# When the weights of the second half are loaded, and phi_q@KV in single tiles instead of pairs: a transformer block with kernel-feature attention

## The chip, the cores and the metric

The kernel runs on one core of a Trainium2 chip. A core has five engines that run side by side and meet through semaphores: TensorE (matmuls; in the profile PE, and PEld for its weight loads), VectorE (DVE), ScalarE (ACT), GpSimd (POOL) and SyncE (SP), which here issues nearly all DMA transfers. Matmuls write to PSUM, eight banks of 2 KB per partition; everything else lives in SBUF, 128 partitions wide. Sixteen DMA engines move the data between DRAM and SBUF, and also the engines' own instructions.

The metric is the device time of one execution in microseconds (us), the median over several executions. A change is called faster or slower against that median. TensorE's clock can be throttled; the profile gives the granted clock as a share of full speed.

## The reference

One sequence of 2048 rows, 640 wide; 32 heads of 20; FFN width 1536; bfloat16.

```python
qkv = layernorm(x) @ wqkv                     # -> q, k, v per head (32 heads of 20)
pq  = einsum("bhsd,hdf->bhsf", q, w_phi)      # the same for k -> pk
phi_q = concat([softmax(pq), softmax(-pq)])   # over f; the same for pk -> phi_k
kv  = einsum("bhsf,bhsd->bhfd", phi_k, v)     # sum over all 2048 rows
z   = einsum("bhsf->bhf", phi_k)
num = einsum("bhqf,bhfd->bhqd", phi_q, kv)
den = einsum("bhqf,bhf->bhq", phi_q, z) + 1e-6
h   = x + (num / den) @ wo
h2  = h + (gelu(layernorm(h) @ w_gate) * (layernorm(h) @ w_up)) @ w_down
```

The attention is linear: every row's phi_k and v are first summed into one small kv matrix per head, and only then can the first row's phi_q be multiplied with it.

## The kernel before, in words

The rows are cut into 16 tiles of 128, and four tiles make a block. The kernel has a first phase, which ends with the sum kv, and a second, which makes attention, W_o and the FFN.

**First phase.** w_phi is folded into the weights of k and q, so that pk and pq come from one matmul each (`fold`, tile names wa, Wk2, Wq2; the q weights come transposed from DRAM as WqT through `load_T`). A loop over the 16 tiles (`for t in range(NT)`) does in pass t: the matmuls pk of tile t and two exponentials on ACT (`k_tile`, E); the matmuls v of tile t+4 (`v_mm`, pv) and their copy out of PSUM on ACT (`v_ev`, vS); the layer norm of tile t+6 on ACT (`ln_ap`) and its transpose by a DMA that SP issues (LN1T); sums, reciprocals and products for phi_k on DVE and POOL (`k_norm`, vt). At passes 5, 9, 13 and 15 some tiles are added up in PSUM (`kv_tile`, kvp): 40 small matmuls of 32 columns each per tile. In pass 15 and behind it 6 tiles, 240 matmuls, stand in a row. Passes 7 to 10 also issue the five transposes of WqT, pass 9 three tiny DMAs (kmask), passes 10 to 14 the five folds for q. In pass 13 SP is given Wg, Wo and Wu, 1920, 800 and 1920 KB, each in one DMA. SP works its list in order: what waits there holds all that is behind it.

**Second phase.** `kv_mask` moves the sum from PSUM to SBUF (KV). Wd, 1920 KB, is issued by SP in two DMAs as soon as the memory of the first phase is free. Blocks of pq (`q_mm`) and their exponentials (`q_exp`, Eq) go on, woven by hand with the attention of tiles 0 and 1. The attention of a tile has stages: `attn_a_mm` (phi_q@KV, 40 matmuls of 32 rows, PSUM tile ab, and the copies to AB), `attn_b`, `attn_b2`, `attn_b3` (divide, on POOL and DVE: pr, den, rd, w, tt, o; then a DMA transpose oT), `attn_c` (po, times Wo), `attn_d` and `attn_d2` (the sum with x, statistics), `attn_e` (layer norm, DMA transpose LN2T).

`weave(units, stages)` sets the order: units are TensorE's long work, `gate_up` (10 matmuls gu, 2.2 us at 512 columns, gelu on ACT, product GT on DVE) and `down` (12 matmuls pd, the sum y on DVE, later a store). A stage with the number i is put ahead of unit i; what lies beyond the last unit goes to the next weave with the number reduced. The second weave has 16 units, the third 20.

From stage 12 of the second weave (`split`) on, the eight PSUM banks are given out one by one in a ring (`bank`): ab takes four, a gu two, a po two, a pd one. Tiles 8 to 15 go through `attn_pair`: ab of two tiles, eight banks, and then the copies of both, two on ACT and two on DVE for each tile. The AB buffers are four.

TensorE's and SP's instructions stay in the order in which they are written; so do those of the other engines (`manual_schedule`).

Of the kernel before, what the change touches and what calls it, by code (L numbers as in the profile page):

```python
# [17 lines left out]
def kernel(  # L18
# [12 lines left out]
    nc = tc.nc  # L31
# [8 lines left out]
    NC = D // P  # L40
    NF = FF // P
# [16 lines left out]
    KC = Dh + 2  # L58
# [3 lines left out]
    QH, QF = H // 4, D // 4  # L62
# [19 lines left out]
    Wo = const.tile([P, NC, D], BF16, name="Wo")  # L82
    Wg = const.tile([P, NC, FF], BF16, name="Wg")
    Wu = const.tile([P, NC, FF], BF16, name="Wu")
    KV = const.tile([P, 2, SL, KC], BF16, name="KV")

    Eq = [const.tile([P, len(g), 2, 512], BF16, name=f"Eq{j}") for j, g in enumerate(QG)]
# [109 lines left out]
    wo_v = A_wo.rearrange("(c p) n -> p c n", p=P)  # L197
    wg_v = B_w_gate.rearrange("(c p) n -> p c n", p=P)
    wu_v = B_w_up.rearrange("(c p) n -> p c n", p=P)
# [68 lines left out]
    def ln_ap(t, on_act=False, on_pe=False):  # L268
        ln = (ln_act if on_act else ln_dve)(p1, "1", *lnp[t])
        if on_pe:  # L270
            lnp[t] = ln
        else:
            transpose_to(LN1T[t // 4][:, :, t % 4 * P:(t % 4 + 1) * P], ln, False)
# [15 lines left out]
    def v_mm(t, us=(0, 1)):  # L289
        if 0 in us:  # L290
            pv[t] = gtile("pv")
        proj(pv[t], t, Wv, us)
# [19 lines left out]
    def k_tile(t):  # L312
        pk = gtile("pk")
        proj(pk, t, Wk2, rows=t == 0)
        Ek[t] = ev.tile([P, 2, D], BF16, name="E", bufs=8)
        for s in range(2):
            nc.scalar.activation(Ek[t][:, s, :].rearrange("p (u f) -> p u f", u=2), pk[:, :, 0:HD],  # L317
                                 ACTF.Exp, scale=((lnp[t][2], nrstd[t]) if t in CT else (1.0, -1.0))[s])
# [45 lines left out]
    def q_mm(j, part=(0, 1)):  # L364

        if 0 in part:
            pqs[j] = gtile("pq")
        for i, bc in enumerate(QG[j]):
            if i not in part:
                continue  # L370
            b, c = divmod(bc, NC)
            for kc in range(NC):
                nc.tensor.matmul(pqs[j][:, i, :], lhsT=Wq2[:, kc, c * P:(c + 1) * P], rhs=LN1T[b][:, kc, :],  # L373
                                 start=(kc == 0), stop=(kc == NC - 1))

    def q_exp(j, signs=(0, 1)):
        for s in signs:
            nc.scalar.activation(Eq[j][:, :, s, :], pqs[j][:, 0:len(QG[j])], ACTF.Exp, scale=(1.0, -1.0)[s])  # L378
# [80 lines left out]
    ev_cm = tc.tile_pool(name="ev", bufs=1, side="right", reuse_waits="tile")  # L459
    ev = ev_cm.__enter__()  # L460

    for t in range(NT):
        if t == T3:
            ps_cm.close()
            psG = ps_cm.enter_context(tc.tile_pool(name="psG", bufs=3, space=PSUM, reuse_waits="tile"))
            psK = ps_cm.enter_context(tc.tile_pool(name="psK", bufs=1, space=PSUM, reuse_waits="tile"))
            kvp = psK.tile([P, 2 * SL, VC], F32, name="kvp")
        k_tile(t)
        if t == 0:
            ln_ap(6)  # L470
        if t in FQ:
            fold(WqT, Wq2, True, [i for i, f in enumerate(FQ) if f == t])
        for j in range(len(QT)):
            if t == QT[j]:
                q_mm(j)
                q_exp(j)
        for i in KVG.get(t, ()):
            kv_tile(i)
        if 0 < t < NT - 4:
            v_mm(t + 4)  # L480
        if t > 0 and t + 6 < NT:
            ln_ap(t + 6, on_act=True)
        if 0 < t < NT - 4:
            v_ev(t + 4)
        if t % 2 == 0 and t + 8 < NT:
            ln_st(t + 8, t + 9)
        k_norm(t)
        load_T(WqT, 0, *[i for i, f in enumerate(LQ) if f == t])
        if t == 10:
            transpose_to(LN1T[0][:, :, P:2 * P], ln_a(1), False)  # L490
        if t == 12:
            ln_ap(0, on_act=True)
        if t == 7:
            nc.gpsimd.memset(kmask[QUAD[0]], 1.0)
            for k, lo, n, base in ((3, 0, 2, 0), (2, 6, 3, 12)):
                m = kmask[QUAD[0], lo:lo + 6].rearrange("p (k n) -> p k n", k=k)
                nc.gpsimd.affine_select(out=m, in_=m, pattern=[[4, k], [-Dh, n]],
                                        compare_op=ALU.is_ge, fill=0.0, base=base, channel_multiplier=1)
                nc.gpsimd.affine_select(out=m, in_=m, pattern=[[-4, k], [Dh, n]],
                                        compare_op=ALU.is_ge, fill=0.0, base=Dh - 1 - base, channel_multiplier=-1)  # L500
        if t == 8:
            nc.gpsimd.memset(KV, 0.0)
        if t == 9:
            for r in (1, 2, 3):
                nc.sync.dma_start(kmask[QUAD[r]], kmask[QUAD[0]])
        if t == 11:
            nc.gpsimd.tensor_copy(KV[:, 0, :, KC - 1], kmask)
            nc.gpsimd.tensor_copy(KV[:, 1, :, 0], kmask)
        if t == 13:
            nc.sync.dma_start(Wg, wg_v)  # L510
            nc.sync.dma_start(Wo, wo_v)
            nc.sync.dma_start(Wu, wu_v)
    q = len(QT)
    for t in range(12, NT):
        kv_tile(t)
# [9 lines left out]
    p2r = ctx.enter_context(tc.tile_pool(name="p2r", bufs=1, side="right", reuse_waits="tile"))  # L525
    Wd = p2r.tile([P, NF, D], BF16, name="Wd")
    wd_v = B_w_down.rearrange("(c p) n -> p c n", p=P)
    for f in (0, NF // 2):
        nc.sync.dma_start(Wd[:, f:f + NF // 2], wd_v[:, f:f + NF // 2])

    ABs = [p2r.tile([P, 2, H, KC], F32, name=f"AB{i}") for i in range(2)]
    ABs += [LN1F[:, i * 2 * H * KC:(i + 1) * 2 * H * KC].rearrange("p (s h f) -> p s h f", s=2, h=H) for i in range(2)]
    LN2T, st = {}, {}
# [9 lines left out]
    def attn_a_mm(t):  # L543

        b = t // 4
        if b not in LN2T:
            LN2T[b] = p2.tile([P, NC, 512], BF16, name="LN2T", bufs=2)
        if psB:
            ab = [bank("ab") for r in range(4)]
        else:  # L550
            st[t, "ab"] = gtile("ab"), gtile("ab")
            ab = [x[:, i] for x in st[t, "ab"] for i in range(2)]
        for s in range(2):
            for c in range(NC):
                i, h, n = SLOT[c]
                h += s * QH
                for r, q in enumerate(QUAD):
                    nc.tensor.matmul(ab[r][:, h * KC:(h + n) * KC], lhsT=eq(t, c, s)[q],  # L558
                                     rhs=KV[q, s, i:i + n].rearrange("p h f -> p (h f)"),
                                     start=(s == c == 0), stop=(s == 1 and c == NC - 1), skip_group_check=True)  # L560
        st[t] = ab

    def attn_pair(t):

        for i in (t, t + 1):
            attn_a_mm(i)
        for i in (t, t + 1):
            AB = ABs[i % len(ABs)]
            for r in range(4):
                (nc.scalar.copy, nc.vector.tensor_copy)[r % 2](  # L570
                    AB[:, :, r * QH:(r + 1) * QH].rearrange("p s h f -> p s (h f)"),
                    st[i][r][:, 0:2 * QH * KC].rearrange("p (s x) -> p s x", s=2))
            st[i] = AB

    def attn_a(t, dve=0):
        attn_a_mm(t)
        AB, ab = ABs[t % 2], st[t, "ab"]
        for u in ((1, 0) if t in (4,) else (0, 1)):
            (nc.vector.tensor_copy if u >= 2 - dve else nc.scalar.copy)(
                AB[:, :, u * UH:(u + 1) * UH].rearrange("p s (r h) f -> p r s (h f)", r=2),  # L580
                ab[u][:, :, 0:2 * QH * KC].rearrange("p r (s x) -> p r s x", s=2))
        st[t] = AB

# [178 lines left out]
    q_mm(q + 2)  # L762
    attn_t(0)
    q_exp(q + 1, (1,))
    q_exp(q + 2, (0,))
    q_mm(q + 3, (0,))
    attn_b(1, True)
# [30 lines left out]
    def attn_at(t, i, offs):  # L798

        fns = (attn_a, attn_b, attn_b2, attn_b3, attn_c, attn_d, attn_d2, attn_e)  # L800
        return [(i + o, fn, t) for fn, o in zip(fns, offs) if o >= 0]

    SHORT = (0, 2, 3, 4, 9, 9, 10, 12)
# [3 lines left out]
    def attn_rest(t, i):  # L807
        return [(i + o, fn, t) for fn, o in zip((attn_b, attn_b2, attn_b3, attn_c, attn_d, attn_d2, attn_e), LONG)]
# [4 lines left out]
          attn_at(2, 0, (-1, 0, 1, 2, 7, 7, 8, 10)) + attn_at(3, 1, (2, 3, 4, 5, 9, 9, 10, 12)) + attn_at(4, 6, SHORT2) + attn_at(5, 9, SHORT2) +  # L813
          attn_at(6, 13, SHORT2))
    weave(gus(0, 256, 512) + downs(0, (2, 3)),
          attn_at(7, 0, SHORT) + [(12, split), (14, attn_pair, 8), (16, attn_pair, 10)] + attn_rest(8, 15) +
          attn_rest(9, 17) + attn_rest(10, 19) + attn_rest(11, 21))
    weave(gus(1, 0, 512) + downs(1, range(4)),
          [(18, attn_pair, 12), (20, attn_pair, 14)] + attn_rest(12, 19) + attn_rest(13, 21) + attn_rest(14, 23) +
          attn_rest(15, 25))  # L820
    for b in (2, 3):
        weave(gus(b, 0, 512) + downs(b, range(4)), [])
# [31 lines left out]
```

## Time and profile before

| | |
|---|---|
| median of 3 runs | 282.93 us (282.88 to 282.96) |
| the profiled execution | 283.22 us, of which the span from first to last instruction is 281.2 us |
| TensorE busy | 270.1 us (96%), mean granted clock 0.987 |
| DVE, ACT, POOL busy | 173.7, 140.4, 96.4 us (62%, 50%, 34%) |
| DMA | 21.46 MB, mean 76 GB/s |
| Wg, Wo, Wu from issue to landing | 9.3, 10.5, 14.8 us |
| Wd, each of two | 7.9 us |
| LN1T, oT, LN2T, each | 2.6 us |

How to read it: the profile names each instruction by engine, line and operation, with output tile <- inputs. "Idle before" is the engine's idle time ahead of an instruction, and after "<-" stands what ended it; "issue" means that nothing the profile shows was being waited for. The slices cut the span in 40 equal parts with the busy share in tenths. The chain of waits goes back from the last instruction to what released it. Matmuls are pipelined and their recorded lengths overlap, so the starts are the better measure. SPq is the time in which SP issued; the transfer follows it.

### The profile page before, as it was taken

The page shows a single profiled execution, that of the slowest core. Times are in us where ns is not written, and L with a number is a line of the kernel's source. Part 1 is how long each engine was busy: PE and PEld are TensorE (multiplying, and loading weights), DVE is VectorE, ACT ScalarE, POOL GpSimd, SP SyncE. Part 2 cuts the span into 40 slices and gives each one's busy share as a digit, 9 for nine tenths or more (in the row PEclk, how much of TensorE's full clock was granted, in tenths as well). Part 3 has the DMA queues.
Part 4 walks back from the last instruction along what each step waited for, and adds up shares of the span by engine and source line. Part 5 has one row for each costly group of instructions (what it writes and reads, how often), then busy time and mean ns, then how long its engine had stood idle before and what let it go on. Part 6 is the DMA issues. An engine that isn't in the chain of part 4 may idle for free.

```text
span 281.2 us, 7231 instructions
## 1 busy us (share of the span) xinstructions
PE 270.1 (96%) x2981; PEld 172.7 (61%) x2995; DVE 173.7 (62%) x332; ACT 140.4 (50%) x241; POOL 96.4 (34%) x218
## 2 busy tenths in 40 slices
PE   7999999998499999999999999999999999999996
PEld 3777777765145688778864555576455567444574
DVE  5899999995068586666558785327776432233232
ACT  5789897887069975545534245404234520222200
POOL 4248898764001123736411383201255210000000
PEclk9999999999689999999999999999999999999999
DMA  7972627699900011324220322210113411000011
GB/s 200 193 244 47 73 57 112 72 233 392 357 7 2 2 24 26 72 50 94 43 55 2 70 48 47 49 48 28 47 23 72 48 47 49 23 0 0 2 47 47
DMA packets 42401, 21.46 MB, mean 76 GB/s; under 512 B 35201, under 2 KB 40577, under 8 KB 42369
## 3 DMA queue, kind: packets, MB, share of 16 engines
q1 hardware_dynamic: 41712, 20.98, 30.9%
q8 instruction: 23, 0.38, 0.6%
q10 hardware_dynamic: 656, 0.03, 0.2%
q14 instruction: 10, 0.07, 0.1%
HBM read 10.18 MB, written 2.62 MB: 46 GB/s over the span
## 4 chain that ended last, share of the span: by engine, by line
PE 87%; DVE 4%; DMA 3%; issue 3%; ACT 2%; SPq 0%; POOL 0%; POOLq 0%
PE gu L692 37%; PE pd L711 19%; PE pq L373 8%; PE po L632 8%; PE pk L284 5%; PE pv L284 4%; PE kvp L351 2%; PE ab L558 2%; DMA Wv<-in_A_wqkv_dram 2%; DMA LN1T<-ln 1%; DVE stats L113 1%; PE wa L237 1%; DVE y L714 1%; ACT vS L304 1%; ACT E L317 1%
## 5 line engine op out<-in xcount | busy, mean ns | idle before, releaser
L695 ACT ACTIVATE g<-gu 128x512 bf16<-128x512 f32 (+1 forms) x60 | 30.7, 512 | 67.7 <-PE gu L692 66.9
L698 DVE TENSOR_TENSOR GT<-gu,g 128x512 bf16<-128x512 f32 (+1 forms) x60 | 34.4, 580 | 48.2 <-PE gu L692 39.3
L692 PE MATMUL gu<-LN2T,Wg 128*128 128x512 bf16 (+1 forms) x291 | 61.3, 335 | 0.5
L692 PE MATMUL gu<-LN2T,Wu 128*128 128x512 bf16 (+1 forms) x300 | 61.8, 336 | 0.0
L711 PE MATMUL pd<-Wd,GT 128*128 128x320 bf16 (+2 forms) x396 | 53.5, 295 | 0.0
L711 PEld LDWEIGHTS <-GT 128*128 128x128 bf16 x396 | 37.9, 98 | 14.6 <-DVE GT L698 0.2
L692 PEld LDWEIGHTS <-Wu 128*128 128x128 bf16 x300 | 29.3, 98 | 22.6
L692 PEld LDWEIGHTS <-Wg 128*128 128x128 bf16 x300 | 28.8, 98 | 21.2
L284 PEld LDWEIGHTS <-LN1T 128*128 128x128 bf16 x290 | 27.8, 98 | 10.7 <-DMA LN1T<-ln 0.2
L714 DVE TENSOR_TENSOR y<-pd,x_sb 128x320 bf16<-128x320 f32 (+2 forms) x29 | 13.9, 480 | 29.0 <-PE pd L711 29.0
L332 POOL TENSOR_TENSOR vt<-vS,rs 128x672 bf16<-128x672 bf16 x22 | 29.2, 1349 | 7.5 <-DVE rs L328 5.2
L373 PE MATMUL pq<-LN1T,Wq 128*128 128x512 bf16 x95 | 24.8, 404 | 5.2 <-issue 5.0
L632 PE MATMUL po<-Wo,oT 128*128 128x320 bf16 x160 | 24.3, 299 | 0.0
L284 PE MATMUL pk<-Wk,LN1T 128*128 128x320 bf16 x160 | 24.2, 299 | 0.0
L324 DVE TENSOR_REDUCE sk<-E 128x64 f32<-128x1280 bf16 x16 | 22.9, 1433 | 0.3 <-ACT E L317 0.3
L378 ACT ACTIVATE Eq<-pq 128x1024 bf16<-128x1024 f32 (+1 forms) x26 | 20.0, 829 | 1.8 <-PE pq L373 1.7
L632 PEld LDWEIGHTS <-oT 128*128 128x128 bf16 x160 | 15.6, 98 | 7.4 <-ACT oT L157 0.5
L284 PE MATMUL pv<-Wv,LN1T 128*128 128x320 bf16 x130 | 19.8, 299 | 0.1
L317 ACT ACTIVATE E<-pk 128x640 bf16<-128x640 f32 x28 | 18.2, 706 | 3.1 <-PE pk L284 3.0
L373 PEld LDWEIGHTS <-Wq 128*128 128x128 bf16 x100 | 9.9, 102 | 16.1 <-issue 7.2
L143 ACT ACTIVATE ln<-x_sb,v,rstd 128x640 bf16<-128x640 bf16 x14 | 12.9, 920 | 11.3 <-POOL v L671 10.8
L609 DVE TENSOR_TENSOR tt<-AB,w 128x1280 bf16<-128x1280 f32 x12 | 17.8, 1485 | 1.0 <-POOL w L602 0.9
(113 smaller groups left out, 287.5 us busy)
## 6 DMA issues: line engine op xcount, KB each, us to landing
out_dram<-y SPq DMA_DIRECT2D x15, 160.0 KB, 1.8
Wg<-in_B_w_gate_dram SPq DMA_DIRECT2D x1, 1920.0 KB, 9.3
Wu<-in_B_w_up_dram SPq DMA_DIRECT2D x1, 1920.0 KB, 14.8
Wd<-in_B_w_down_dram SPq DMA_DIRECT2D x2, 960.0 KB, 7.9
x_sb<-in_A_x_dram SPq DMA_DIRECT2D x2, 640.0 KB, 6.7
Wo<-in_A_wo_dram SPq DMA_DIRECT2D x1, 800.0 KB, 10.5
x_sb<-in_A_x_dram SPq DMA_DIRECT2D x4, 160.0 KB, 4.2
Wv<-in_A_wqkv_dram SPq DMA_DIRECT2D x2, 320.0 KB, 5.0
```

The source lines that it names most:

```text
L284: nc.tensor.matmul(ps[:, u, 0:HD], lhsT=lnT(t, c), rhs=W[:, c, u * HD:(u + 1) * HD], start=(c == 0), stop=(c == NC - 1))
L317: nc.scalar.activation(Ek[t][:, s, :].rearrange("p (u f) -> p u f", u=2), pk[:, :, 0:HD], ACTF.Exp, scale=((lnp[t][2], nrstd[t]) if t in C ...
L324: nc.vector.reduce_sum(sk, Ek[t].rearrange("p s (h f) -> p (s h) f", f=Dh), axis=AX.X)
L332: eng.tensor_tensor(vt[:, s], vS[t % 8], rs[:, s * H:(s + 1) * H, None].to_broadcast([P, H, VC]), ALU.mult)
L373: nc.tensor.matmul(pqs[j][:, i, :], lhsT=Wq2[:, kc, c * P:(c + 1) * P], rhs=LN1T[b][:, kc, :], start=(kc == 0), stop=(kc == NC - 1))
L378: nc.scalar.activation(Eq[j][:, :, s, :], pqs[j][:, 0:len(QG[j])], ACTF.Exp, scale=(1.0, -1.0)[s])
L609: nc.vector.tensor_tensor(tt.rearrange("p s (h f) -> p s h f", f=Dh), num, w[:, :, :, None].to_broadcast([P, 2, H, Dh]), ALU.mult)
L632: nc.tensor.matmul(pos[u], lhsT=st[t][:, c, :], rhs=Wo[:, c, u * HD:(u + 1) * HD], start=(c == 0), stop=(c == NC - 1))
L692: nc.tensor.matmul(gu[i][:, 0:n], lhsT=W[:, c, f * P:(f + 1) * P], rhs=LN2T[b][:, c, a0:a1], start=(c == 0), stop=(c == NC - 1))
L695: nc.scalar.activation(g[:, 0:n], gu[0][:, 0:n], ACTF.Gelu_apprx_tanh)
L698: nc.vector.tensor_tensor(st[b, "g", f][:, a0:a1], gu[1][:, 0:n], g[:, 0:n], ALU.mult)
L711: nc.tensor.matmul(ps, lhsT=st[b, "g", f][:, tl * P:(tl + 1) * P], rhs=Wd[:, f, f0:f1], start=(f == 0), stop=(f == NF - 1))
```

## The change

Wg and Wu are no longer loaded by one DMA each in pass 13, but in five pieces of 384 KB each, with Wo between them, one DMA at the end of each pass 0 to 10. Wd's two DMAs move behind the exponentials of the second pq block of the second phase; to hold them there, POOL copies two elements of that block's Eq into Wd first, so that the DMAs, which overwrite them, must wait. And tiles 8 to 15 go through `attn_one`, a tile at a time: tile 8 at stage 14 of the second weave, 9 at 16, 10 at 18, 11 at 20, and tiles 12 to 15 at 18, 20, 22 and 24 of the third. The other stages of these tiles keep their numbers.

```diff
+    wload = [(W[:, c], v[:, c]) for W, v in ((Wg, wg_v), (Wu, wu_v)) for c in range(NC)]
+    wload.insert(NC, (Wo, wo_v))
 
     for t in range(NT):
...
-        if t == 13:
-            nc.sync.dma_start(Wg, wg_v)
-            nc.sync.dma_start(Wo, wo_v)
-            nc.sync.dma_start(Wu, wu_v)
+        if t < len(wload):
+            nc.sync.dma_start(*wload[t])
...
-    for f in (0, NF // 2):
-        nc.sync.dma_start(Wd[:, f:f + NF // 2], wd_v[:, f:f + NF // 2])
+
+    def load_wd(j):
+
+        nc.gpsimd.tensor_copy(Wd[:, 0:NF:NF // 2, 0], Eq[j][:, 0, 1, 0:2])
+        for f in (0, NF // 2):
+            nc.sync.dma_start(Wd[:, f:f + NF // 2], wd_v[:, f:f + NF // 2])
...
-    def attn_pair(t):
-
-        for i in (t, t + 1):
-            attn_a_mm(i)
-        for i in (t, t + 1):
-            AB = ABs[i % len(ABs)]
-            for r in range(4):
-                (nc.scalar.copy, nc.vector.tensor_copy)[r % 2](
-                    AB[:, :, r * QH:(r + 1) * QH].rearrange("p s h f -> p s (h f)"),
-                    st[i][r][:, 0:2 * QH * KC].rearrange("p (s x) -> p s x", s=2))
-            st[i] = AB
+    def attn_one(t):
+
+        attn_a_mm(t)
+        AB = ABs[t % len(ABs)]
+        for r in range(4):
+            (nc.scalar.copy, nc.vector.tensor_copy)[r % 2](
+                AB[:, :, r * QH:(r + 1) * QH].rearrange("p s h f -> p s (h f)"),
+                st[t][r][:, 0:2 * QH * KC].rearrange("p (s x) -> p s x", s=2))
+        st[t] = AB
...
     q_exp(q + 1, (1,))
+    load_wd(q + 1)
     q_exp(q + 2, (0,))
...
-          attn_at(7, 0, SHORT) + [(12, split), (14, attn_pair, 8), (16, attn_pair, 10)] + attn_rest(8, 15) +
+          attn_at(7, 0, SHORT) + [(12, split), (14, attn_one, 8), (16, attn_one, 9), (18, attn_one, 10), (20, attn_one, 11)] + attn_rest(8, 15) +
           attn_rest(9, 17) + attn_rest(10, 19) + attn_rest(11, 21))
...
-          [(18, attn_pair, 12), (20, attn_pair, 14)] + attn_rest(12, 19) + attn_rest(13, 21) + attn_rest(14, 23) +
+          [(18, attn_one, 12), (20, attn_one, 13), (22, attn_one, 14), (24, attn_one, 15)] + attn_rest(12, 19) + attn_rest(13, 21) + attn_rest(14, 23) +
           attn_rest(15, 25))
```

## The prediction

> **What bounds the kernel now.** I read the slices first, then TensorE's timeline, then the chain, then SP's queue. The page gives, over 40 slices of 7.03 us, TensorE's busy tenths, its granted clock and the DMA engines' share, and the queue that carries instructions:
>
> ```profile
> PE   7999999998499999999999999999999999999996
> PEclk9999999999689999999999999999999999999999
> DMA  7972627699900011324220322210113411000011
> q8 instruction: 23, 0.38, 0.6%
> ```
>
> TensorE is the bound: 9 tenths everywhere but slices 10 and 11, and there its clock falls too, while DMA is full. TensorE's timeline (start, length, operation, idle before) shows the hole:
>
> ```profile
> 67.36 2.14 PE L351 MATMUL kvp<-vt,E 128*32 128x42 bf16 x240
> 74.24 0.61 PE L373 MATMUL pq<-LN1T,Wq 128*128 128x512 bf16 x1 [4.74 <-issue]
> 75.06 3.62 PE L373 MATMUL pq<-LN1T,Wq 128*128 128x512 bf16 x8 [0.22 <-issue]
> 78.62 0.63 PE L558 MATMUL ab<-KV,Eq 32*128 32x44 bf16 x40
> 99.50 0.46 PE L558 MATMUL ab<-KV,Eq 32*128 32x44 bf16 x40
> 99.89 0.72 PE L692 MATMUL gu<-LN2T,Wg 128*128 128x256 bf16 x5
> ```
>
> After 240 small matmuls TensorE stands still for 4.74 us, and "issue" says that no semaphore held it. Its instructions did: q8 brought 0.38 MB in 23 packets, 16 KB each, and 5,976 matmuls and weight loads over 23 packets make 260 instructions a packet. The burst's 480 instructions take 2.1 us, so they use up almost two packets. The DMA view of 71.6 to 72.8 us (queue, packets, MB, share) has the one that was missing; none lies between 68.0 and 71.6:
>
> ```profile
> q8 instruction: 1, 0.02, 5.7%
> ```
>
> It starts at 71.65, takes 1.09, and TensorE goes on 1.5 us after it. Meanwhile the 16 engines move Wg, Wo, Wu (issued from 57.14) and Wd (from 69.62). The clock pays as well (window, ..., PEclk, DMA share, GB/s):
>
> ```profile
> 69.50:72.50 3.00, 0.00 (x1) 0.00 (x0) 0.88 (x2) 0.00 (x0) 0.00 (x0) 1.00 1.03 381
> 72.50:79.40 6.90, 4.94 (x50) 1.95 (x52) 0.01 (x1) 0.08 (x1) 0.00 (x0) 0.51 0.74 251
> ```
>
> The chain (start, length, what) has two more places, one in the loop over tiles and one at the pairs:
>
> ```profile
> 27.23 4.08 DMA LN1T<-ln
> 31.40 1.53 PE pv L284 x10
> ...
> 142.97 0.02 issue
> 142.99 0.50 DVE y L714
> 143.50 0.04 issue
> 143.54 0.45 PE ab L558 x35
> ```
>
> **The change, part by part.** The sum is made against the profiled execution, 283.22 us, 0.29 above the runs' median of 282.93.
>
> (a) *The hole.* Without bulk loads beside it, the eighth packet comes sooner. In earlier bursts of the same matmuls, q8's packet started 2.0 us after the burst's start (42.37, packet 44.41) and 1.5 after (55.09, packet 56.57); here 4.3 after 67.36. So it starts at 68.9 to 69.4; with its 1.09 and the tail of 1.5 TensorE goes on at 71.4 to 72.0; if the tail was stretched by the full engines too (transposes land about 0.4 after their last packet), at 70.3. I take 71.4: 2.8 us gained. Ends: 0 (74.24 as now) and 4.3 (70.0). The vector work on KV is over at 70.5 and is not needed before ab.
>
> (b) *The clock.* From 72.5 to 79.4 it is half. The 5.13 us of work from 74.24 to 79.37 would take 2.57. An idle stretch of 2 instead of 4.7 us should not drop it: I take 2.6. Ends: 0 and 2.6.
>
> (c) *Pairs to singles.* A pair needs all eight PSUM banks, so its second half waits for the y of the matmuls just ended (the 0.50 in the chain). The four pairs run 142.89 to 143.92 and 147.28 to 148.38 and again so at 189.59 and 193.98: 1.03, 1.10, 1.03, 1.10, 4.26 us. A lone ab takes 0.39 (99.50 to 99.89); eight take 3.1 to 3.2. Gain 1.1. A single takes four banks, whose last readers are two units (over 4 us) back; evictions of 0.46 (ACT) and 0.51 (DVE), the same number as before, now lie at units 14, 16, 18, 20 and 18 to 24. In the units with both AB evictions and tt, DVE has some 5.9 us per two units against TensorE's 6.1 with po; behind it queue GT and so the gu banks. Who waits on a later AB: POOL's pr of tile 9, now one unit (2.2) behind its ab instead of three, and five units on its po; POOL stands idle there up to 4.76 (before w at 150.0). Should the DVE cover fail, half the gain goes: ends 0.5 and 1.7 (the 0.33 before each second half and 0.18 twice).
>
> (d) *Eleven pieces in the loop*, ten of 384 KB and Wo's 800 KB, behind LN1T's transposes in SP's queue. On SP each costs about 0.45 (the x_sb loads' 0.43). On the engines a piece needs 1.0 us at the 384 GB/s of the bulk load. LN1T transposes are issued 2.6 to 3.8 us apart, have their packets 1.2 to 2.1 after issue and land after 2.6; a piece issued behind one runs about 2.5 to 3.5 after it, just ahead of the next one's packets. That fits, but with little air: v of tile 7 starts 0.3 after its landing, tiles 8 and 12 0.4 and 0.5, tile 9 waits already (31.31, then 31.40), held up 1.5 us by an instruction packet at 28.2. Every such wait is lost, since TensorE never idles from 31.4 to 67. The pieces are in by about 57; gu first reads them at 96, po at 85. Then SP's queue:
>
> ```profile
> 42.05 1.20 SPq L159 DMA_TRANSPOSE LN1T<-ln  x1
> 43.30 1.27 SPq L194 DMA_TRANSPOSE WqT<-in_A_wqkv_dram  x1
> 44.67 2.08 SPq L159 DMA_TRANSPOSE LN1T<-ln  x1
> 46.79 2.59 SPq L194 DMA_TRANSPOSE WqT<-in_A_wqkv_dram  x2
> 49.48 3.35 SPq L505 DMA_DIRECT2D kmask<-kmask  x3
> 52.88 1.28 SPq L194 DMA_TRANSPOSE WqT<-in_A_wqkv_dram  x1
> 54.27 2.82 SPq L159 DMA_TRANSPOSE LN1T<-ln  x2
> ```
>
> It is back to back from 42 to 55.5. Three pieces go ahead of the last WqT: 3 x 0.45 less 0.3 of slack makes it 1.1 late; it landed at 55.92 and its fold starts at 58.02. Behind a piece and an instruction packet (1.0, 1.4) it may be late by up to 1.4. LN1T of tile 0 landed at 59.40 and is first needed at about 61.9. I take 0.3 for tile 9 and 0.3 for the fold: 0.6 lost. Ends: 0, and 2.4: 1.5 more on every transpose (the collision's row) against the loop's own cycle, in which landing, v 1.36, k 1.36, two E 1.31 and ln 0.81 close in three passes, 8.16 us, so 3.3 is free, 0.8 is lost per round, three rounds.
>
> (e) *Wd later.* One tiny POOL copy (the 128x12 copy took 0.24) behind the second exponential of block q+1, about 79, on a POOL with nothing to do until 98; then two issues, 0.95, on an SP idle until 102. Wd lands after 7 to 9 us, before 90, and is first read at 113.5 less the shift. The next instruction packets have over 10 us to spare there. Cost 0; if POOL or SP were held, Wd has 15 us before it shows.
>
> Sum: -2.8 - 2.6 - 1.1 + 0.6 = -5.9: 277.3 profiled, 277.0 as median.
>
> **Two rules against it.** The Trainium skill (Runtime: NRT & Kernel Launch, Instruction fetch mechanics) gives TensorE an instruction memory of 128 KiB refilled in 16 KiB blocks, the cost mostly hidden. By it the hole is no fetch, and (a) and (b) vanish: 282.4. The 16 KB packets agree; the hole that ends behind one does not. The Trainium skill (DMA: Bandwidth & Descriptors, Rules for kernel authors) wants 1 MiB or more per DMA and names a fixed 2 us each; eight more DMAs would be 16 us if they lay on the path, and the sum would end near 293. The three-pass slack says they mostly do not.
>
> **Rivals.** *Clock drops anyway* (0.12): two idle microseconds fill over half of some 3.4 us stretch, and the half clock lasted two of these (6.83). Then (b) is 0: about 279.6. For it: one drop is all the trace shows. *Pieces collide with every transpose* (0.10): (d) at 2.4, 278.8, to 280.5 if half as much again. Against: 1.0 us of DMA work in 2.7 us passes with a share of 0.2 to 0.7. *The hole stays* (0.07): whatever ended it at 74.24 was not the load beside it; 283 - 1.1 + 0.6 = 282.4. *Slower* (0.10): SP. If rings that are full hold SP at each piece as at kmask's first issue (2.10 of the 3.35, for 0.8 KB), three pieces make the last WqT 6.0 late, the fold stalls 3.9, and such a gap halves the clock for 2.6 as in (b): 6.5, the whole gain. From 2.1 us per piece it decides; at 2.4 the time is 284. Against: Wo and Wu, issued right behind Wg, took 0.51 and 0.52.
>
> **How the numbers follow.** Forecast 0.61, 275.6 to 278.5 by itself. The range 275.5 to 280.8 takes in the clock and the collisions. 0.2% (0.57 us) is what this measurement can tell from no change. Faster 0.85, same 0.04 (half of the hole that stays, and mixtures), slower 0.11.
>
> **What would show it.** Right: the wait before pq after the 240 kvp matmuls near 2 us, PEclk without 6 and 8, no 0.50 of y before ab, DMA tenths of slices 3 to 7 higher and 8 to 11 low. Wrong: idle before v of tiles 7 to 9 or 12, or before wa at about 58; a half clock at another place; LN1T landing over 3.3 after issue.

## The result, and the profile after

The changed kernel takes 280.81 us (279.40 to 281.55, six executions) against 282.94 before: ratio 0.9923, interval 0.9894 to 0.9951. It is faster, by 2.1 us instead of 5.9. The forecast's direction held; its size did not, and 280.81 lies just above the range's end of 280.8.

The profiled execution has 281.55 us, 1.67 less than that of before, with a span of 279.6. TensorE's busy tenths, its clock and the DMA share over 40 slices of 6.99 us:

```profile
PE   8999989999699999999999999999999999999996
PEclk9999999999899999999999999999999999999999
DMA  6968999780006211314211222210213411000011
```

The hole has shrunk to one slice of 6 tenths, and the bulk of the DMA work lies in slices 3 to 9. TensorE's timeline (start, length, operation, idle before) marks three waits in the loop, and the hole:

```profile
27.62 1.53 PE L284 MATMUL pv<-Wv,LN1T 128*128 128x320 bf16 x10 [0.22 <-DMA LN1T<-ln]
31.77 1.53 PE L284 MATMUL pv<-Wv,LN1T 128*128 128x320 bf16 x10 [0.40 <-DMA LN1T<-ln]
41.28 1.53 PE L284 MATMUL pv<-Wv,LN1T 128*128 128x320 bf16 x10 [1.18 <-DMA LN1T<-ln]
...
69.14 2.14 PE L351 MATMUL kvp<-vt,E 128*32 128x42 bf16 x240
73.69 3.77 PE L373 MATMUL pq<-LN1T,Wq 128*128 128x512 bf16 x10 [2.41 <-issue]
77.39 0.60 PE L563 MATMUL ab<-KV,Eq 32*128 32x44 bf16 x40
```

The three waits are v of tiles 8, 9 and 12 behind their transposes. Beside the hole the DMA engines carry nothing but instruction packets: two between 68 and 76 us, in slices of 0.2 us, the first of them the eighth, from 71.05, 1.9 us after the burst's start:

```profile
DMA  0000000000000003000000000000000000300000
q8 instruction: 2, 0.03, 1.8%
```

The clock (window, PE, PEld, DVE, ACT, POOL busy, PEclk, DMA share, GB/s) still halves, for 3.41 us instead of 6.83:

```profile
71.01:74.43 3.42, 1.01 (x38) 0.55 (x25) 0.88 (x2) 0.08 (x1) 0.00 (x0) 1.00 0.02 5
74.43:77.84 3.41, 3.41 (x48) 1.23 (x46) 0.00 (x0) 0.00 (x0) 0.00 (x0) 0.50 0.02 5
```

The same matmuls' starts in both traces give the account:

| stretch | before, us | after, us | difference |
|---|---|---|---|
| start to pk of tile 2 | 20.83 | 20.45 | -0.38 |
| from there to the 240 kvp matmuls | 46.53 | 48.69 | +2.16 |
| from there to the first ab of the second phase | 11.26 | 8.25 | -3.01 |
| of this, to the restart at pq | 6.88 | 4.55 | -2.33 |
| of this, pq to ab, mostly at half clock | 4.38 | 3.70 | -0.68 |
| first ab to po of tile 8 (tiles 8 to 11) | | | -0.19 |
| po of tile 8 to po of tile 12 (tiles 12 to 15) | | | -0.24 |

The first row is no part of the change: the traces of the four kernels below that leave this stretch alone (e2, e3, e6, e10) are 0.28 to 0.46 early as well. The rest says it: 3.0 us won at the hole, 0.4 at the tiles, 2.2 lost in the loop.

### The profile page after: what moved, and what is told of

It is laid out like the page before. It is cut to its first block, busy times and chain, and to the rows that moved or that the text cites. A ratio compares the mean times of both kernels' runs of the same rounds, so it can differ in the third digit from the quotient of the medians.

```text
span 279.6 us, 7257 instructions
## 1 busy us (share of the span) xinstructions
PE 271.6 (97%) x2995; PEld 172.6 (62%) x2995; DVE 173.1 (62%) x332; ACT 140.8 (50%) x241; POOL 95.7 (34%) x219
## 4 chain that ended last, share of the span: by engine, by line
PE 84%; DMA 4%; ACT 4%; DVE 3%; issue 3%; POOL 0%; ACTq 0%; POOLq 0%
PE gu L695 38%; PE pd L714 19%; PE po L635 8%; PE pq L373 6%; PE pk L284 4%; DMA LN1T<-ln 3%; PE pv L284 3%; PE ab L563 2%; PE kvp L351 2%; PE tp L156 1%; DVE stats L113 1%; ACT E L317 1%; DMA x_sb<-in_A_x_dram 1%; PE wa L237 1%; ACT ln L143 1%
```

## The experiments

**Theory.** The hole is instructions that come too late: a burst of 480 outruns the packets of 260, and the bulk load makes the packet later still. The loop's loss comes from weight pieces ahead of transposes that have little slack, Wo's 800 KB above all. **Rivals:** Wd at the hole's start is what delayed the packet; something behind the last kvp matmul holds pq; an instruction packet that falls on tile 12's transpose makes it late, or any piece in the loop costs.

Each time is a median; before had 282.77, 282.83 and 282.39 beside the three groups e1 to e4, e5 to e8, e9 and e10. The changed kernel was not run again in these groups, so differences from its 280.81 are between groups.

### The parts one by one

e1: the pieces alone.

```diff
+        if t < len(wload):
+            nc.sync.dma_start(*wload[t])
-        if t == 13:
-            nc.sync.dma_start(Wg, wg_v)
...
```

> The kernel before with the pieces of Wg, Wo, Wu in passes 0 to 10 alone; Wd and the pairs as before. Theory (the load of Wg, Wo, Wu beside the instruction packet made the hole long; the pieces cost in the loop): v of tiles 8, 9 and 12 wait 0.4, 0.6 and 1.3 us, some 2.2 us lost in the loop against before; TensorE's wait ahead of pq behind the 240 kvp matmuls is 2.4 to 2.6 us, although Wd is issued as it begins, since the instruction packet starts some 1.9 us after the burst, ahead of Wd's packets; time 280.8 to 281.6. Rival (Wd, issued at the hole's start, delayed the packet): the wait stays over 4 us, time 283 to 285.

280.72, ratio 0.9917 (0.9890 to 0.9944). TensorE's timeline of e1, its waits:

```profile
27.71 1.53 PE L284 MATMUL pv<-Wv,LN1T 128*128 128x320 bf16 x10 [0.28 <-DMA LN1T<-ln]
41.59 1.53 PE L284 MATMUL pv<-Wv,LN1T 128*128 128x320 bf16 x10 [1.82 <-DMA LN1T<-ln]
73.37 1.94 PE L373 MATMUL pq<-LN1T,Wq 128*128 128x512 bf16 x5 [2.00 <-issue]
```

The pieces alone bring both the loss and the gain. Tile 9 did not wait here, tile 12 waited longer; the hole is 2.0 with Wd issued as it begins.

e2: Wd later alone.

```diff
-    for f in (0, NF // 2):
-        nc.sync.dma_start(Wd[:, f:f + NF // 2], wd_v[:, f:f + NF // 2])
+    def load_wd(j):
...
     q_exp(q + 1, (1,))
+    load_wd(q + 1)
```

> The kernel before with Wd later alone. Theory: Wg, Wo and Wu still fill the DMA engines until 73.5, so the instruction packet is as late and the wait ahead of pq stays 4.5 to 4.8 us, the clock halves for 6.8 us; 282.6 to 283.1, no change. Rival (Wd is what delayed the packet, or the 1.5 us between the packet and the restart): wait 2.5 to 3.5, time 279 to 281.

282.94, ratio 0.9998 (0.9979 to 1.0017). The hole in e2's timeline:

```profile
73.85 0.61 PE L373 MATMUL pq<-LN1T,Wq 128*128 128x512 bf16 x1 [4.64 <-issue]
```

Wd's place shows no effect, in either direction, within about half a microsecond, and the hole stays. The rival that names it falls.

e3: singles alone.

```diff
-          [(18, attn_pair, 12), (20, attn_pair, 14)] + ...
+          [(18, attn_one, 12), (20, attn_one, 13), (22, attn_one, 14), (24, attn_one, 15)] + ...
```

> The kernel before with single tiles alone. Theory (a single ab among gu costs 0.4 to 0.5 us, since the wide matmul behind it starts 0.1 to 0.2 late; eight singles 3.8 against 4.26 for the pairs): 0.45 us gained, 282.4 to 282.6. Rival (0.39 each, as the prediction had it): 1.1 gained, 281.8.

281.89, ratio 0.9971 (0.9949 to 0.9993). The interval, 0.2 to 1.4 us, holds both figures; the trace decides. Against before, po of tile 7 starts 0.65 earlier, of tile 8 0.91, of tile 12 1.16: the four pairs give 0.26 and 0.25. The missing half shows in the changed kernel's timeline:

```profile
145.47 0.47 PE L563 MATMUL ab<-KV,Eq 32*128 32x44 bf16 x40
145.97 1.24 PE L695 MATMUL gu<-LN2T,Wg 128*128 128x512 bf16 x5
...
148.13 1.24 PE L695 MATMUL gu<-LN2T,Wg 128*128 128x512 bf16 x5
149.21 1.24 PE L695 MATMUL gu<-LN2T,Wu 128*128 128x512 bf16 x5
150.38 0.47 PE L563 MATMUL ab<-KV,Eq 32*128 32x44 bf16 x40
150.78 1.25 PE L695 MATMUL gu<-LN2T,Wg 128*128 128x512 bf16 x5
```

From its own start to the next start an ab takes 0.40 in six of the eight singles, ahead of pd, po or gu alike, and 0.50 and 0.47 in the two between pd and gu (145.47 and 191.95). The eight make 3.36 against the pairs' 4.26, which is 0.90 less. But an ab also starts late behind the matmuls ahead of it: five gu take 1.08 from start to start, and 1.17 where an ab follows (149.21 to 150.38). This 0.1 is paid ahead of each of the eight singles, and was paid ahead of only four pairs: 0.4 of the 0.9 is lost again, and 0.5 is left. So the expectation had the size, 0.45, and the wrong place for most of it. No wait for banks or copies was left.

By their medians the three parts add to 3.2 us, and the whole change gave 2.1. Each of these figures is uncertain by 0.5 to 0.8 us, so this does not show that the parts disturb each other.

### The loop

e4: Wo behind pass 13.

```diff
-    wload.insert(NC, (Wo, wo_v))
+    wload.extend([None] * 3 + [(Wo, wo_v)])
...
+        if t < len(wload) and wload[t]:
```

> The changed kernel with Wo taken out of pass 5 and put behind pass 13; Wg's pieces stay in passes 0 to 4, Wu's in 5 to 9. Theory (Wo's 800 KB, 2.1 us and more on the engines, hold LN1T of tile 12 behind them): v of tile 12 waits 0.2 us or less instead of 1.35, about 1.2 us gained on the changed kernel, 279.0 to 280.2. Rival (the instruction packet that falls on that transpose does it): the wait stays over 0.8 us, time 280.5 to 281.3.

278.62, ratio 0.9872 (0.9828 to 0.9915). Tile 12 still waits, a third of it:

```profile
39.91 1.53 PE L284 MATMUL pv<-Wv,LN1T 128*128 128x320 bf16 x10 [0.41 <-DMA LN1T<-ln]
```

0.41, more than the 0.2 expected, but far under the rival's 0.8. The rival does not fall by that: here the instruction packet ran from 35.77 to 37.37 and was gone when tile 12's transpose had its first packets, 1.17 us after its issue at 36.24, so this run took away both Wo and the packet. The 2.2 us on the changed kernel are more than the loop's gain (kvp's burst starts 1.37 earlier): the clock did not fall in this trace, though the hole was as long (2.42).

e10: Wo alone in pass 5, on the kernel before.

```diff
+        if t == 5:
+            nc.sync.dma_start(Wo, wo_v)
         if t == 13:
             nc.sync.dma_start(Wg, wg_v)
-            nc.sync.dma_start(Wo, wo_v)
```

> The kernel before with Wo alone moved to pass 5; Wg and Wu at 13 as before. Theory (Wo needs over 3 us on the engines there, not the 2.1 of the bulk load, and holds the transpose of tile 12): v of tile 12 waits 0.7 to 1.5 us, tiles 7 and 8 not at all; the hole is as long as before, since 3.8 MB still load beside it; 283.0 to 284.3. Rival (the ten other pieces ahead of it made tile 12 late): no wait there, 282.3 to 283.

281.25, ratio 0.9954 (0.9925 to 0.9984): outside both expectations.

```profile
40.81 1.53 PE L284 MATMUL pv<-Wv,LN1T 128*128 128x320 bf16 x10 [1.54 <-DMA LN1T<-ln]
...
73.06 2.33 PE L373 MATMUL pq<-LN1T,Wq 128*128 128x512 bf16 x10 [2.54 <-issue]
```

The first half holds: Wo moved alone, without the ten pieces, makes tile 12 wait 1.54 us. The second does not: the hole is short although Wg and Wu, 3.8 MB, still load beside the burst. That load moved 405 GB/s from 66 to 69.5; from 70.5 to 72 the engines moved 77 GB/s, and the packet started at 70.68, 2.30 us after the burst's start: with 0.8 MB less and a burst 1.0 us later, the load had all but run out. In before it ran on past 71.65, the packet's start there. This fits a packet that is delayed by what is still under way when it is asked for; how an engine chooses between the two queues was not measured.

Why Wo was so costly shows in the changed kernel's SP queue, and in the windows (columns as above) over which Wo's packets ran:

```profile
32.68 1.22 SPq L159 DMA_TRANSPOSE LN1T<-ln  x1
33.94 0.78 SPq L513 DMA_DIRECT2D Wo<-in_A_wo_dram  x1
36.83 1.21 SPq L159 DMA_TRANSPOSE LN1T<-ln  x1
38.09 0.58 SPq L513 DMA_DIRECT2D Wu<-in_B_w_up_dram  x1
```

```profile
35.30:36.50 1.20, 1.20 (x11) 0.88 (x9) 1.10 (x2) 1.20 (x3) 1.20 (x2) 1.00 0.50 58
36.50:38.60 2.10, 2.10 (x18) 1.49 (x17) 2.10 (x8) 2.08 (x4) 2.10 (x2) 1.00 1.02 363
```

Wo moved 58 GB/s in its first 1.2 us and 363 after that (384 from 36.8 to 38.4, the rate of the bulk load). So its rows of 1280 bytes were not slower than the weights' 3072 once it ran; what the bulk rate leaves out is the start. Wg's one DMA in the kernel before starts so too, 164 GB/s from 58.9 to 60.4 and then 417, while Wo directly behind another load, in e7, moved 373 from 62.7 to 64.9. Why a load starts slowly was not measured.

Tile 12's transpose, issued at 36.83, had its first packets at 38.45 instead of 1.2 after issue, an instruction packet fell on it at 38.45, and it landed after 4.40 instead of 2.6. Such a packet alone can do most of this: on tile 9's transpose before, at 28.2, it cost 1.5. In e5 tile 12's transpose had its first packets on time, 1.18 after issue, with an instruction packet on it from 38.16 to 39.32, and v still waited:

```profile
40.94 1.53 PE L285 MATMUL pv<-Wv,LN1T 128*128 128x320 bf16 x10 [0.85 <-DMA LN1T<-ln]
```

In all four traces with Wo in pass 5 (after, e1, e5, e10) an instruction packet overlaps tile 12's transpose, and in after and e5 it starts only as Wo's last packets leave, some 3 us later than in before (35.44). So e4 and e10 show that Wo in pass 5 brings the wait; how much of it comes from Wo's own packets, and how much from the instruction packet beside or behind them, they do not separate.

e7: another schedule. Nothing ahead of the transposes of tiles 8 and 9, and the last two pieces of Wu and Wo at 13.

```diff
+    for t, w in zip((0, 3, 4, 5, 6, 7, 8, 10, 13, 13, 13), order):
+        wload.setdefault(t, []).append(w)
```

> The changed kernel with the loads at other passes: Wg's pieces at 0, 3, 4, 5, 6, Wu's first three at 7, 8, 10, and Wu's last two and Wo at 13. None goes ahead of the transposes of tiles 8 and 9, and Wo's 800 KB of none in the loop; the last three are done by 65, before the burst. Theory (the loop's loss comes from pieces ahead of transposes with little slack): waits before v together under 0.6 instead of 2.3, hole as in the changed kernel (2.4), 278.3 to 279.5. Rival (any piece in the loop costs, through SP's issue or the engines): the loss stays over 1.5, 280 to 281.

278.27, ratio 0.9856 (0.9830 to 0.9883). One wait is left in the loop, now tile 14, and the hole:

```profile
47.37 1.53 PE L284 MATMUL pv<-Wv,LN1T 128*128 128x320 bf16 x10 [0.37 <-DMA LN1T<-ln]
...
72.00 2.33 PE L373 MATMUL pq<-LN1T,Wq 128*128 128x512 bf16 x10 [2.43 <-issue]
```

The burst starts at 67.44, 1.70 before the changed kernel's. Eight pieces in the loop left one wait here. Two of them still go ahead of transposes with little slack, those of tiles 7 and 12, which did not wait in this trace; so slack is a good guide, but this run alone does not prove it.

### The hole

e5 and e6: the 240 matmuls spread over the pq blocks of pass 15, on the changed kernel and on the one before.

```diff
+    SPREAD = ((10, 11), (12,), (13,), ())
...
                 q_mm(j)
                 q_exp(j)
+                for i in SPREAD[j]:
+                    kv_tile(i)
...
-    for t in range(12, NT):
+    for t in range(14, NT):
         kv_tile(t)
```

> The changed kernel with the 240 kvp matmuls spread: tiles 10 and 11 behind the first of the four pq blocks of pass 15, 12 behind the second, 13 behind the third, 14 and 15 at the end, where TensorE goes on with pq as before. Same matmuls, same data, 80 small ones in a row instead of 240. Theory (TensorE stands still because 480 instructions in 2.1 us outrun the packets of 260): the wait ahead of pq falls from 2.4 to under 0.6 us, no half clock; 2.4 us and, where the clock fell, 1.7 more: 276.5 to 278. Rival (something behind the last kvp matmul, its sum or its PSUM, holds pq): the wait stays 2.0 to 2.6, time 280 to 281.5.

> The same spreading on the kernel before, with the bulk loads still there. Theory (an instruction packet beside the full load takes 3.4 from request to start, 1.1, and 1.5 to the restart, 6 us; from 59.7 to 69.5 some 560 instructions go by, 2.2 packets, one per 4.5 us): waits of 1 to 3 us remain, now ahead of other matmuls, 278.5 to 281. Rival (the load is no matter once the burst is gone): no waits, no half clock, 275.5 to 276.5, which would beat the change without moving a load.

e5: 278.43, ratio 0.9843 (0.9819 to 0.9867), a little over the 276.5 to 278 expected. Its last burst, of 80, and what follows:

```profile
70.62 0.80 PE L352 MATMUL kvp<-vt,E 128*32 128x42 bf16 x80
72.11 2.32 PE L374 MATMUL pq<-LN1T,Wq 128*128 128x512 bf16 x10 [0.68 <-ACT Eq L379]
```

pq still follows the last kvp matmul, but the wait on nothing is gone. In its place stands a known one, 0.68 for an exponential on ACT, a little over the 0.6 expected. The clock stays full. Nothing behind kvp held pq for 2.4 us; that rival falls.

e6: 280.97, ratio 0.9925 (0.9897 to 0.9952):

```profile
66.56 0.82 PE L374 MATMUL pq<-LN1T,Wq 128*128 128x512 bf16 x3 [0.26 <-issue]
...
72.76 3.96 PE L374 MATMUL pq<-LN1T,Wq 128*128 128x512 bf16 x10 [3.05 <-issue]
```

With the bulk load the spread burst still ends in a wait of 3.05, mostly at the old place. Burst and load are both needed to explain the 4.74: taking away the load leaves 2.4, taking away the burst leaves 3.3, taking away both leaves none of it. The clock was at half for one stretch of 3.41 us in this trace; the rival, by which the load is no matter, falls.

e8: both, the schedule of e7 and the spread.

> Both: the loads at those passes, and the kvp matmuls spread. If both theories hold, the gains add: 278.9 less 2.4 for the hole and up to 1.7 for the clock, 275 to 276.5. If the spread waits for the products vt of tiles 12 and 13 instead, or if the loads of pass 13 hold an instruction packet, 277 to 279.

277.54, ratio 0.9819 (0.9794 to 0.9844), 5.3 us under before and 3.3 under the changed kernel's median. The gains do not add in full, and the time lies in the second of the expected ranges, for another reason than those named there: ACT's wait of 0.69 ahead of pq takes the hole's place, and v of tiles 7, 12 and 14 waited 0.35, 0.19 and 0.16 in the trace. It is below both kernels' medians.

e9: no load in passes 0 and 5.

```diff
-    for t, w in zip((0, 3, 4, 5, 6, 7, 8, 10, 13, 13, 13), order):
+    for t, w in zip((3, 4, 6, 7, 8, 10, 11, 13, 13, 13, 13), order):
```

> As the schedule with spread matmuls, with no load at passes 0 and 5: Wg's pieces at 3, 4, 6, 7, 8, Wu's at 10 and 11, its last three and Wo at 13. Theory (only pieces issued ahead of a transpose with under 0.6 us of slack cost, tiles 7, 8, 9 and 12): no wait over 0.2 ahead of v of these tiles, 0.3 to 0.8 less than with passes 0 and 5: 276.8 to 277.3. Rival (loads at 13 reach into the pq blocks and hold an instruction packet, or the waits move to tiles 13 and 14): 277.4 to 278.5.

277.58, ratio 0.9833 (0.9799 to 0.9867): the rival's case, no gain on e8. Its waits:

```profile
47.82 1.53 PE L285 MATMUL pv<-Wv,LN1T 128*128 128x320 bf16 x10 [0.62 <-DMA LN1T<-ln]
...
68.30 0.82 PE L374 MATMUL pq<-LN1T,Wq 128*128 128x512 bf16 x3 [0.72 <-issue]
```

Tiles 7, 8, 9 and 12 no longer wait; tile 14 does, and with the loads of pass 13 the instruction wait is back, inside a pq block.

## Why the prediction was wrong, point by point

**(a) the hole: mechanism right, a little long.** 2.33 us gained, 2.8 forecast. The eighth packet started 1.9 us after the burst's start, within the 1.5 to 2.0 read from earlier bursts; the 2.8 took the early end of these. What I had left open was the tail: TensorE restarted 1.50 us after the packet's end before, and 1.47 after it here, 1.48 in e1, 1.47 in e7. It is not stretched by the load, so the upper end of (a), 4.3, was never there. The rival that the hole stays did not come.

**(b) the clock: a step that failed.** I took all 2.57 us, and 0.68 were gained. From the restart at pq to the first tp behind the two ab it takes 9.88 us before, 9.20 after, and 7.64 in e4, e7 and e10, whose clock stayed full there: the half clock cost 2.24 before, not 2.57, and 1.56 of it was still lost after. "An idle stretch of 2 instead of 4.7 us should not drop it" was an assumption; the rival that named what happened, an idle stretch that fills over half of some 3.4 us, got 0.12. Four of the six executions of the changed kernel show a mean clock of 0.993 to 0.994 and take 280.43 to 281.55 us; two show 1.0 and take 279.40 and 280.08. So the half clock seems to be in four of the six; that it depends on where the idle stretch falls is argued below, from the traces of several kernels.

**(c) the pairs: mis-sized.** 0.43 to 0.5 instead of 1.1. I priced a single by its own start and the next, 0.39; the eight came to 3.36, a little over the 3.1 to 3.2. What the sum had at nothing is that an ab starts 0.1 late behind the matmuls ahead of it, eight times for singles and four for pairs: 0.4 us (e3). The row used for the price stands behind such a delay too: 0.65 from the last gu at 98.85 to the ab at 99.50, where gu otherwise takes 0.55. The lower end, 0.5, was right, for another reason than the one given for it.

**(d) the pieces: the step that cost most.** 2.16 us lost, 0.6 forecast; the upper end of 2.4 held it. Of the sum's terms, tile 9 was 0.36 beyond its wait of before (0.3 forecast), tile 8 cost 0.38 and tile 12 1.35 (0 and 0 forecast). "A piece needs 1.0 us" was the price of 384 KB in the middle of a bulk load. Wo's 800 KB got no price of its own; at that rate it is 2.1 us, and it ran for 3.3, with 58 GB/s in its first 1.2. And an instruction packet, which I had counted at tile 9 and at the fold only, fell on tile 12's transpose as well; how much of the 1.35 each of the two made is open. The fold of WqT, where I put the other 0.3, never waited: its last transpose was issued at 55.02 instead of 52.88, and the fold itself came at 59.80 instead of 58.02, because the loop was late.

**(e) Wd: right.** e2 shows no difference. The POOL copy came at 85.16, later than "about 79", and nobody waited for it.

**The two rules.** The Trainium skill (Runtime: NRT & Kernel Launch, Instruction fetch mechanics) has the cost of a refill mostly hidden; here TensorE waited for one packet alone in each of the two traces, and that one wait is 4.74 us before and 2.41 after. e5 removes it by order alone. The Trainium skill (DMA: Bandwidth & Descriptors, Rules for kernel authors) prefers 1 MiB or more per DMA; in e7 eight pieces of 384 KB in the loop left one wait of 0.37.

**Chances and range.** The sum took the clock at its good end and the other terms on the good side of what came. The clock that falls (0.12) and the pieces that collide (0.10) were priced one at a time, and the range did not hold both at their ends: 277.0 + 2.6 + 1.8 is 281.4, over 280.8. (The 280.5 for collisions half as dear again should be 280.0.) They came together, with singles at half: -2.3 - 0.7 - 0.4 + 2.2 = -1.2, and -0.4 from the start. The slower rival, SP held by full rings, came only in small: a piece's issue took 0.58 instead of 0.45.

## What to carry to other kernels

A wait that the profile gives to nothing, behind a run of very small matmuls, should be checked against the queue that carries instructions: here the same matmuls in another order ended it. A load that is moved out of one stage has to be priced in the stage that receives it, with its start as well as its rate, and by the slack of each transfer queued behind it, one by one. And a range that is said to hold two rivals has to be added up with both of them in it.

## What was not expected

**The clock is decided window by window.** In the traces it changes only at times that lie whole multiples of 3.41 us apart. TensorE's busy time in the window that holds the idle stretch, read from windows laid on those multiples, sorts the kernels: 0.36 us (before), 1.01 (after), 1.36 (e1) were followed by a half clock; 1.93 (e4) and 2.17 (e7) were not. In this order, with both windows of e4 and e7 (same columns as above; after's stands with the result):

```profile
69.14:72.55 3.41, 0.36 (x45) 0.26 (x32) 0.88 (x2) 0.17 (x1) 0.00 (x0) 1.00 1.03 382
70.82:74.23 3.41, 1.36 (x71) 0.85 (x59) 0.87 (x2) 0.36 (x1) 0.00 (x0) 1.00 0.42 104
67.98:71.39 3.41, 1.93 (x236) 1.83 (x220) 0.88 (x2) 1.74 (x3) 0.00 (x0) 1.00 0.02 5
71.39:74.81 3.42, 2.43 (x41) 1.12 (x43) 0.00 (x0) 0.00 (x0) 0.00 (x0) 1.00 0.02 5
67.41:70.82 3.41, 2.17 (x241) 2.04 (x240) 0.87 (x2) 1.97 (x4) 0.01 (x1) 1.00 0.02 5
70.82:74.24 3.42, 2.23 (x10) 0.90 (x10) 0.00 (x0) 0.00 (x0) 0.00 (x0) 1.00 0.02 5
```

e7's hole of 2.43 us is cut in two by the border, and each part leaves TensorE busy for over 60% of its window. After's of 2.41 fell into one window, and the next was halved. So a wait of 2.4 us costs 2.4 or some 4.0 (with the 1.56 above), by where it lies. e2, e3 and e6 fit as well: 0.10, 1.02 and 0.45 us of work, and a half clock after each. The limit lies between 1.36 and 1.93 us, as far as these traces tell; no run was made to find it. The Trainium skill (TensorE: Matmul & The Clock Gate, What's actually happening) gives such a free-running window of 3413 ns, which agrees; its section Why this matters for your kernels warns of gaps over about 3 us, and here 2.0 (e1) was enough.

**A packet's 16 KB cost more than their transfer.** It takes 0.9 to 1.7 us on its engine, and in the hole TensorE restarts 1.3 to 1.5 us after its end (before, after, e1, e4, e7, e10), with the DMA engines full or empty. So even with no weights loading beside it, the burst of 240 was followed by a wait of 2.0 to 2.4 us (after, e1, e4, e7).
